# A transformer block's opening re-laid: the condition vector in eight rows, a small load moved, and a planner that may let two engines idle

## Chip, core and metric

The kernel runs on one core of one Trainium2 chip. The metric is the device time of one execution in microseconds (us); three runs of the kernel before gave 2205.80, 2207.83 and 2208.32, so a median of 2207.83. The engines are called as the profile calls them: PE (TensorE matmul; PEld is its weight load), DVE (VectorE), ACT (ScalarE), POOL (GpSimd), SP (SyncE, which issues all DMAs here).

## What is computed

One transformer block with adaptive layer norm. A condition vector `c` (1024 values) goes through silu and a matrix `w_mod` to six vectors that scale, shift and gate two halves: an attention half with 32 heads of 32 channels in four segments of 512 tokens with a running memory between them, and a token-mixing MLP half.

```python
x = A_x                                                     # (1, 2048, 1024)
mod = (_silu(c) @ w_mod).reshape(c.shape[0], 6, 1, -1)
sa, ca, ga, sb, cb, gb = (mod[:, i] for i in range(6))
h = _layernorm(x, axis=-1) * (1 + ca) + sa
x = x + ga * _A_ref(h, A_wq, A_wk, A_wv, A_wo, A_beta)
h = _layernorm(x, axis=-1) * (1 + cb) + sb
x = x + gb * _B_ref(h, B_w1, B_b1, B_w2, B_b2)
...
# in _A_ref, with g = _sigmoid(beta), one value for each head, and for each segment:
p = _softmax(logits, axis=-1); a_dot = p @ vs
o = g * (pq @ M) / (pq @ z + 1e-6) + (1.0 - g) * a_dot
M = M + pk.T @ vs; z = z + sum(pk)
```

## The kernel before

Products of fp32 operands are made as three products of fp32r halves: a helper (`split`, lines 105 to 116) writes a rounded high part (ACT, L113, or DVE, L115) and the remainder as low part (DVE or POOL, L116).

**The opening** (lines 257 to 298) does segment 0. It loads four tiles of x (L198), normalizes them in two pairs (`norm_tiles`, L205 to L222: bn_stats and bn_aggr on DVE, L212 and L213; two small ACT steps for the inverse root, L215 and L216; four small DVE steps, L217 to L220; then the scaling of each whole tile on ACT, L222). `c` comes as a 128 x 8 tile `csb` (L98), goes through silu (L99 to L103), is spread to a 128 x 1024 tile `bc` (L262), which eight PE transposes (L266) and two ACT copies (L267) turn into `scb`, in which every partition holds the whole silu(c). For each of eight chunks `ct` of 128 channels, two tiles `wm` of w_mod (512 KB each, L284) are multiplied with `scb` and summed on DVE (L285), which gives shift and scale `saca` of the chunk (L288 adds one). `h_chunk` (L224) transposes the four x tiles' columns of the chunk on PE (L227), applies scale and shift on ACT (L229) and splits the result; `first_chunk` then multiplies it with the first two head groups' weights (L182 for keys and values, L190 for queries). These weights arrive as `raw` tiles (L144) and are split. The products of all chunks go to six PSUM banks that stay open.

**The gate**: beta (32 values) is loaded to all 128 partitions (`gate`, L300, a DMA that reads the same 128 B for each partition), goes through a sigmoid on ACT and DVE (L301 to L304), and POOL makes from it eight masks `bdg` (L318 and L321, one pair for each head group), with which the memory update is multiplied when it goes into `MZ` (L429, L432). The second part of the gate (1 - g) is used where the values are scaled (L505).

**Pools**: `st1` holds the opening's tiles (x, `bc`, eleven buffers of `wm`, `h32`). `prj`, `late` and the two `sk` pools are laid over the same space once `st1` is closed, and wait tile by tile for what lay there. `gate` is in `top`, on the other side of the memory, where nothing has to be waited for.

**The order**: `set_order` hands the whole program, some 38,000 instructions, to a planner (class `Order`). It has a cost for each instruction (`cost`, `transfer`), goes through the program forward in modelled time (`forward`), then backward to get due times, three times over, and fixes the order of the instructions on each engine, SP's DMAs among them. In `forward`, `pick` takes the engine that can start something soonest and gives it the ready instruction with the smallest key (its due time); an engine does not stay idle while it has something ready (large DMAs behind a backlog apart). Each engine works its instructions off in that fixed order, so that an instruction that waits holds up what stands behind it.

Of the kernel before, what the change touches and what calls it, by code (L numbers as in the profile page):

```python
# [9 lines left out]
F32 = mybir.dt.float32  # L10
# [3 lines left out]
AF = mybir.ActivationFunctionType  # L14
ALU = mybir.AluOpType
# [4 lines left out]
S, D, H, DH, F = 2048, 1024, 32, 32, 3584  # L20
P = 128
NSEG, L = 4, 512
NK = D // P
# [21 lines left out]
def attention_and_mlp(ctx, tc, x, wq, wkv, wo, beta, w1, b1, w2, b2, c, wm_a, wm_b, out):  # L45
    nc = tc.nc
    V, A, G, T, SY = nc.vector, nc.scalar, nc.gpsimd, nc.tensor, nc.sync
# [13 lines left out]
    const = ctx.enter_context(tc.tile_pool(name="const", bufs=1))  # L61
# [9 lines left out]
    top = top_pool.__enter__()  # L71
# [4 lines left out]
    def bank(tag, bufs, name):  # L76
# [3 lines left out]
    ident = top.tile([P, P], F32, name="ident")  # L80
# [5 lines left out]
                    channel_multiplier=1)  # L86
# [8 lines left out]
    G.memset(eps, EPS)  # L95

    csb = acst.tile([P, 2, NK], F32, name="csb")
    SY.dma_start(csb[:, 0], c)  # L98
    A.activation(csb[:, 1], csb[:, 0], AF.Exp, scale=-1.0)  # L99
    V.tensor_scalar_add(csb[:, 1], csb[:, 1], 1.0)  # L100
    V.reciprocal(csb[:, 1], csb[:, 1])
    sc = const.tile([P, NK], F32, name="sc")
    V.tensor_mul(sc, csb[:, 0], csb[:, 1])  # L103

    saca = acst.tile([P, NK, 2], F32, name="saca")
    MZ = acst.tile([P, NG, 132], F32, name="MZ")
    bdg = acst.tile([P, NG, 132], F32, name="bdg")
# [150 lines left out]
    left = tc.tile_pool(name="st1", bufs=1)  # L258
    s1p = left.__enter__()
    xs = {0: [load_x(s1p, tt) for tt in range(4)]}  # L260
    bc = s1p.tile([P, NK, P], F32, name="bc")
    V.tensor_copy(bc, sc.unsqueeze(2).to_broadcast([P, NK, P]))  # L262
    for i in range(2):
        ps = bank("pj", 2, f"scps{i}")
        for j in range(4):
            T.transpose(ps[:, 128 * j:128 * j + 128], bc[:, 4 * i + j], ident)  # L266
        A.copy(scb[:, 512 * i:512 * i + 512], ps)  # L267
    first = [[bank("pj", 2, "nps0_0"), bank("pj", 2, "nps0_1"), bank("s1", 2, "qps0")],
             [bank("pv", 1, "nps1_0"), bank("ms", 1, "nps1_1"), bank("s1", 2, "qps1")]]
# [26 lines left out]
    norm_tiles(s2p, xs[1])  # L296
    for ct in range(NK):
        h_chunk(s2p, xs[1], 1, ct)
    gate = top.tile([P, 3, H], F32, name="gate")
    SY.dma_start(gate[:, 0], bass.AP(tensor=beta.tensor, offset=beta.offset, ap=[[0, P], [1, H]]))  # L300
    A.activation(gate[:, 1], gate[:, 0], AF.Exp, scale=-1.0)  # L301
    V.tensor_scalar_add(gate[:, 1], gate[:, 1], 1.0)
    V.reciprocal(gate[:, 0], gate[:, 1])
    V.tensor_scalar(gate[:, 1], gate[:, 0], -1.0, 1.0, op0=ALU.mult, op1=ALU.add)  # L304

    left.__exit__(None, None, None)
    prj = tc.tile_pool(name="prj", bufs=1, reuse_waits="tile")
    pj = prj.__enter__()
# [1 line left out]
    b = late.__enter__()  # L310
# [3 lines left out]
    skt = [[q.tile([98, 2, L], F32R, name=f"sk{i}_{h}") for h in range(4)] for i, q in enumerate(sk_)]  # L314
    for sk in skt[0] + skt[1]:
        G.memset(sk[96:98, 1].bitcast(F32), 1.0)
    for g in range(NG):
        G.tensor_tensor(bdg[:, g, 0:128].rearrange("p (h e) -> p h e", h=4),  # L318
                        bd[:, 0:128].rearrange("p (h e) -> p h e", h=4),
                        gate[:, 0, 4 * g:4 * g + 4].unsqueeze(2).to_broadcast([P, 4, 32]), op=ALU.mult)  # L320
        G.tensor_copy(bdg[:, g, 128:132], bd[:, 128:132])  # L321
# [283 lines left out]
    for n in range(-LEADS, 4 * NI + VL):  # L605
# [4 lines left out]
        if 0 <= m + 4 < 4 * NI:  # L610
            t = (m + 4) // 4
# [8 lines left out]
        if 4 * NI - 5 <= m < 4 * NI + 3:  # L620
            i = m - 4 * NI + 5
# [242 lines left out]
    for u, (ph, g) in enumerate(units):  # L864
# [59 lines left out]
        t = tp.tile([P, 3, 512], F32, tag="tu", bufs=1, name=f"tu{g}")  # L924
# [32 lines left out]
LATEB = 3000.0  # L957
HOLD = 1000.0
EARLY = 60000.0
STAY = 3000.0  # L960
SLACK = 1.06
DMA_SPREAD = 7000.0
# [115 lines left out]
class Order:  # L1078
# [182 lines left out]
    def forward(self, key):  # L1261
        n, E = len(self.X), self.E
        key = [-1e18 if i in self.follows else k for i, k in enumerate(key)]
# [8 lines left out]
        ready, start, fin, seq = [0.0] * n, [0.0] * n, [0.0] * n, []  # L1272
        free, heap, future, link = defaultdict(float), defaultdict(list), defaultdict(list), 0.0
# [9 lines left out]
        def add(i):  # L1283
# [10 lines left out]
            x = self.X[i]  # L1294
            more = HOLD if self.side(x) and ready[i] > EARLY else 0.0
            heapq.heappush(future[E[i]], (ready[i] + more, i))
# [9 lines left out]
                add(i)  # L1306
        while len(seq) < n:
            t, e, i = self.pick(free, heap, future, key)
            x = self.X[i]
            if x.opcode == "DMACopy" and size_of(x.outs[0]) > BULK and link - t - ISSUED > BACKLOG:  # L1310
                heapq.heappush(future[e], (link - ISSUED - BACKLOG, i))
                continue
            if e == "DVE" and self.C[i][2] and port > t + 300 and AVOID and heap[e]:
                near = [(k, j) for k, j in heap[e] if not self.C[j][2] and k < key[i] + AVOID]
                if near:
                    k, j = min(near)
                    heap[e].remove((k, j))
                    heap[e].append((key[i], i))
                    heapq.heapify(heap[e])
                    i, x = j, self.X[j]  # L1320
            if e == "PE":
                f = form(x)
                turn = TURNS.get(last + f, 0)
                if turn > MINT and heap[e] and i not in self.follows:
                    near = [(TURNS.get(last + form(self.X[j]), 0), k, j) for k, j in heap[e] if k < key[i] + STAY]
                    if near and min(near)[0] < turn:
                        turn, k, j = min(near)
                        heap[e].remove((k, j))
                        heap[e].append((key[i], i))
# [24 lines left out]
            for s in strong[i]:  # L1354
                done(s, t if E[s] == e == "PE" else fin[i] + WAKE.get(E[s], 30.0))
            for s in weak[i]:
                done(s, t + 1)
            for tl in tiles_of[i]:
                left[tl] -= 1
                freed[tl] = max(freed[tl], fin[i] + FREED)  # L1360
                if not left[tl]:
                    tag = self.tag_of[tl]
                    heapq.heappush(slots[tag], (freed[tl], tl))
                    again, parked[tag] = parked[tag], []
                    for s in again:
                        add(s)
# [104 lines left out]
```

## Time and profile before

| | |
|---|---|
| median of three runs | 2207.83 us |
| the profiled execution | 2210.61 us, its span 2208.9 us |
| mean granted TensorE clock | 0.998 |
| DVE busy | 1732.7 us (78%) |
| ACT busy | 1097.1 us (50%) |
| POOL busy | 725.7 us (33%) |

The span is from the first to the last record of the profiled execution; its own time has 1.7 us around the span. Times in the rows are from the span's start. A row of the timeline gives start, busy time, engine, line, operation, output and inputs, and in brackets how long the engine had been idle before and what ended that. A row of the stretches gives for each engine the busy time and the number of instructions, then the granted clock, the DMA engines' busy share and GB/s.

### The profile page before, as it was taken

What the parts mean: (1) busy time and instruction counts of PE and PEld (TensorE: products, weight loads), DVE (VectorE), ACT (ScalarE), POOL (GpSimd) and SP (SyncE); (2) the same over time, 40 slices, a digit from 0 to 9 for tenths busy, and PEclk for the clock granted to TensorE, in tenths of its full rate; (3) what the DMA queues carried; (4) which work ended last, traced back from release to release, by engine and by line L of the source; (5) the groups of instructions that cost most, each with busy time, mean ns of one, the idle gap of its engine ahead of it and who ended that gap; (6) DMA issues with size and microseconds to landing.
All of it is one profiled execution on the core that took longest, in us unless ns stands there. A gap on an engine that the chain in (4) does not pass through costs nothing.

```text
span 2208.9 us, 38272 instructions
## 1 busy us (share of the span) xinstructions
PE 2162.7 (98%) x13738; PEld 1876.5 (85%) x13738; DVE 1732.7 (78%) x3818; ACT 1097.1 (50%) x2008; POOL 725.7 (33%) x827
## 2 busy tenths in 40 slices
PE   6999999999999999989999999999999999999999
PEld 6899998989988999878878888888888888888887
DVE  8777777867787756678997555898889787878787
ACT  5688787566666665653443333633334242424232
POOL 3376676476777755551001000043321000000000
PEclk9999999999999999999999999999999999999999
DMA  9666676796777644664467555775549241414134
GB/s 370 189 204 189 192 223 196 244 288 201 224 213 235 181 135 107 191 211 157 139 238 277 191 194 197 276 278 200 201 175 337 86 157 58 149 53 148 58 124 152
DMA packets 174897, 421.74 MB, mean 191 GB/s; under 512 B 17492, under 2 KB 71796, under 8 KB 165748
## 3 DMA queue, kind: packets, MB, share of 16 engines
q1 hardware_dynamic: 174708, 419.30, 57.9%
q8 instruction: 109, 1.79, 0.3%
q14 instruction: 80, 0.66, 0.1%
HBM read 242.00 MB, written 126.37 MB: 167 GB/s over the span
## 4 chain that ended last, share of the span: by engine, by line
PE 83%; DVE 7%; POOL 2%; DMA 2%; ACT 2%; issue 1%; SPq 0%; DVEq 0%; POOLq 0%; ACTq 0%
PE mx L787 46%; PE nps L182 13%; PE qps L190 6%; PE po L688 4%; PE pv L498 4%; POOL ph L484 2%; PE a L469 1%; PE sz L445 1%; PE sx L445 1%; PE rd L417 1%; PE up L427 1%; PE a L472 1%; PE a L475 1%; PE sy L445 1%; PE ops L513 1%
## 5 line engine op out<-in xcount | busy, mean ns | idle before, releaser
L787 PE MATMUL mx<-bU,sp 128*128 128x512 f32 x2352 | 533.7, 389 | 0.9 <-DVE bU L116 0.9
L787 PEld LDWEIGHTS mx<-bU,sp 128*128 128x128 f32 x2352 | 441.3, 188 | 93.2 <-DVE bU L116 1.3
L113 ACT CAST sp<-wr 128x384 fp32r<-128x384 f32 (+2 forms) x408 | 218.4, 545 | 474.3 <-PE mx L787 386.8
L182 PE MATMUL nps<-wv,h 128*128 128x256 f32 x3072 | 444.8, 284 | 0.8 <-POOL h L116 0.6
L787 PE MATMUL mx<-bA,sp 128*128 128x512 f32 x1764 | 433.5, 389 | 1.6 <-ACT cc L792 0.7
L484 POOL TENSOR_TENSOR ph<-p,ph 128x640 f16<-128x640 f32 x256 | 385.3, 1524 | 110.1 <-ACT ph L482 109.0
L182 PEld LDWEIGHTS nps<-wv,h 128*128 128x128 f32 x3072 | 405.6, 189 | 7.0 <-POOL h L116 0.8
L787 PEld LDWEIGHTS mx<-bA,sp 128*128 128x128 f32 x1764 | 330.4, 188 | 72.7 <-ACT cc L792 1.3
L116 DVE TENSOR_TENSOR sp<-wr,sp 128x384 fp32r<-128x384 f32 (+2 forms) x408 | 260.4, 646 | 60.6 <-ACT sp L113 60.1
L794 DVE TENSOR_TENSOR ac<-mx,ac 128x512 f32<-128x512 f32 x280 | 190.7, 688 | 94.6 <-PE mx L787 93.4
L190 PE MATMUL qps<-h,wq 128*128 128x512 f32 x768 | 198.7, 400 | 0.1
L482 ACT CAST ph<-p 128x1280 f16<-128x1280 f32 x128 | 161.4, 1261 | 52.5 <-POOL p L480 51.5
L688 PE MATMUL po<-wo,ots 128*128 128x512 f32 x768 | 182.4, 392 | 0.5 <-ACT mv L125 0.5
L480 POOL TENSOR_SCALAR_AFFINE_SELECT p<-p 128x256 f32<-128x256 f32 x256 | 117.6, 469 | 188.8 <-ACT p L477 94.8
L688 PEld LDWEIGHTS po<-wo,ots 128*128 128x128 f32 x768 | 143.6, 189 | 29.8 <-ACT mv L125 0.9
L190 PEld LDWEIGHTS qps<-h,wq 128*128 128x128 f32 x768 | 140.8, 190 | 29.7 <-PE sz L445 0.5
L787 PE MATMUL mx<-bB,sp 128*128 128x512 f32 x588 | 165.9, 389 | 0.0
L446 DVE CUSTOM_DVE_ANT_0 sx<-sx,mask 128x128 f32<-128x128 f32 (+1 forms) x256 | 110.9, 434 | 69.6 <-PE sx L445 68.9
L659 POOL TENSOR_TENSOR tu<-cc 128x512 f32<-128x512 f32 x14 | 19.1, 1364 | 399.5 <-DVE cc L923 372.1
L787 PEld LDWEIGHTS mx<-bB,sp 128*128 128x128 f32 x588 | 110.4, 188 | 23.0
L498 PE MATMUL pv<-vp,ph 128*128 128x97 bf16 (+1 forms) x2560 | 117.1, 200 | 1.7 <-DVE am L505 1.0
L794 DVE TENSOR_TENSOR cc<-mx,cc 128x512 f32<-128x512 f32 x140 | 95.2, 684 | 25.6 <-PE mx L787 22.0
(179 smaller groups left out, 3258.3 us busy)
## 6 DMA issues: line engine op xcount, KB each, us to landing
sk<-sg SPq DMA_DIRECT2D x384, 128.0 KB
wr<-in_w_dram SPq DMA_DIRECT2D x28, 1024.0 KB
wr<-in_w_dram SPq DMA_DIRECT2D x32, 768.0 KB
bstu<-ucd SPq DMA_DIRECT2D x28, 768.0 KB
wv<-wsp SPq DMA_DIRECT2D x36, 512.0 KB
wsp<-wv SPq DMA_DIRECT2D x32, 512.0 KB
rawm<-in_wm_b_dram SPq DMA_DIRECT2D x32, 512.0 KB
pcd<-cc SPq DMA_DIRECT2D x14, 1024.0 KB
```

The lines of the kernel that those rows point to most:

```text
L113: A.copy(hi, src)
L116: lo_eng.tensor_tensor(lo, src, hi.bitcast(F32), op=ALU.subtract)
L182: T.matmul(ps[:, aa], h[:, j, 128 * tt:128 * tt + 128], wt[:, i, o:o + 256], start=(n == 0), stop=(n >= 6 * NK - 2), skip_group_check=True)
L190: T.matmul(ps, wt[:, i, o:o + 128], h[:, j], start=(k + n == 0), stop=(3 * k + n == 3 * NK - 1))
L446: V.tensor_tensor_reduce(o, o, mask[:, 384 - 128 * i:], 1.0, -3.0e38, op0=ALU.add, op1=ALU.max, accum_out=mx[:, h % 2, i:i + 1])
L480: G.affine_select(w, w, pattern=[[0, 2], [1, 128]], compare_op=ALU.is_ge, fill=0.0, base=0, channel_multiplier=-1)
L482: A.copy(ph[:, 0], p32)
L484: G.tensor_tensor(ph[:, 1, c], p32[:, c], ph[:, 0, c], op=ALU.subtract)
L498: T.matmul(pv[:, i, 0:w], ph[:, part, o:o + 128], d["vp"][:, j, h, 0:w], start=(n == 0), stop=(n == 19), skip_group_check=True)
L688: T.matmul(ps, os_[:, i, P * ct:P * ct + P], wop[ct, nh][:, j], start=(n == 0), stop=(n == 3 * NK - 1))
L787: T.matmul(ps, ops[q][:, i, P * k:P * k + P], b[:, j], start=(m == 0 and first), stop=(m == 3 * nk - 1), skip_group_check=True)
L794: V.tensor_tensor(d, ps, d, op=ALU.add)
```

## The change

`c` is now handed over as eight rows of 128 (`NK` is 8, `P` is 128) and is loaded to eight partitions (`cr`); the silu runs on 8 x 128 elements in place. POOL makes a selector `sel`, of which block k has ones in row k and zeros elsewhere; eight matmuls of a selector block with `cr` put each row of c to all partitions, into the same PSUM banks as before. The `c` load stands behind the four x loads in the program text (the planner sets the real order). `bc` and its copy go.

The gate, its load and its sigmoid move behind the opening, and its tile from the pool `top` to the pool `late`, which lies over the opening's tiles.

In the planner's `forward`, for the first 30 us of modelled time, DVE (up to 200 ns) and ACT (up to 100 ns) pass over the instruction that they have ready, if within that time another one becomes ready whose key is smaller by more than 200 ns and which is ready before the passed-over one would be through.

```diff
-    csb = ...; SY.dma_start(csb[:, 0], c)
-    A.activation(csb[:, 1], csb[:, 0], AF.Exp, scale=-1.0)
-    V.tensor_scalar_add(csb[:, 1], csb[:, 1], 1.0)
-    V.reciprocal(csb[:, 1], csb[:, 1])
-    sc = const.tile([P, NK], F32, name="sc")
-    V.tensor_mul(sc, csb[:, 0], csb[:, 1])
...
     xs = {0: [load_x(s1p, tt) for tt in range(4)]}
-    bc = s1p.tile([P, NK, P], F32, name="bc")
-    V.tensor_copy(bc, sc.unsqueeze(2).to_broadcast([P, NK, P]))
+    sel = s1p.tile([NK, NK, P], F32, name="sel")
+    G.memset(sel, 1.0)
+    G.affine_select(sel, sel, pattern=[[-1, NK], [0, P]], compare_op=ALU.is_equal, fill=0.0, base=0, channel_multiplier=1)
+    cr = s1p.tile([NK, 2, P], F32, name="cr")
+    SY.dma_start(cr[:, 0], c)
+    A.activation(cr[:, 1], cr[:, 0], AF.Exp, scale=-1.0)
+    V.tensor_scalar_add(cr[:, 1], cr[:, 1], 1.0)
+    V.reciprocal(cr[:, 1], cr[:, 1])
+    V.tensor_mul(cr[:, 0], cr[:, 0], cr[:, 1])
     for i in range(2):
         ps = bank("pj", 2, f"scps{i}")
         for j in range(4):
-            T.transpose(ps[:, 128 * j:128 * j + 128], bc[:, 4 * i + j], ident)
+            T.matmul(ps[:, 128 * j:128 * j + 128], sel[:, 4 * i + j], cr[:, 0], start=True, stop=True)
         A.copy(scb[:, 512 * i:512 * i + 512], ps)
...
-    gate = top.tile([P, 3, H], F32, name="gate")     # load and sigmoid, ahead of the pools prj and late
...
+    gate = b.tile([P, 3, H], F32, name="gate")       # the same load and sigmoid, in the pool late, ahead of bdg
...
+EAGER = 200.0
+WD, WA = 200.0, 100.0
+SOON = 30000.0
+WAIT = {"DVE": WD, "Activation": WA}
...
             t, e, i = self.pick(free, heap, future, key)
+            soon = WAIT.get(e, 0.0) if t < SOON else 0.0
+            if soon and future[e] and future[e][0][0] <= t + soon:
+                near = [(key[j], r, j) for r, j in future[e] if r <= t + soon]
+                k, r, j = min(near)
+                if k < key[i] - EAGER and r < t + self.C[i][0]:
+                    heapq.heappush(heap[e], (key[i], i))
+                    free[e] = r
+                    continue
...
-        "c": f("c").reshape(NK, P).T,
+        "c": f("c").reshape(NK, P),
```

More of the change, by code (lines that the diff above doesn't have):

```diff
@@ L97, in attention_and_mlp @@
     csb = acst.tile([P, 2, NK], F32, name="csb")
-    SY.dma_start(csb[:, 0], c)
-    A.activation(csb[:, 1], csb[:, 0], AF.Exp, scale=-1.0)
-    V.tensor_scalar_add(csb[:, 1], csb[:, 1], 1.0)
-    V.reciprocal(csb[:, 1], csb[:, 1])
-    sc = const.tile([P, NK], F32, name="sc")
-    V.tensor_mul(sc, csb[:, 0], csb[:, 1])
     saca = acst.tile([P, NK, 2], F32, name="saca")
@@ L298, in attention_and_mlp @@
         h_chunk(s2p, xs[1], 1, ct)
-    gate = top.tile([P, 3, H], F32, name="gate")
[L300 to L304, printed above, removed]
     left.__exit__(None, None, None)
@@ L316, in attention_and_mlp @@
         G.memset(sk[96:98, 1].bitcast(F32), 1.0)
+    gate = b.tile([P, 3, H], F32, name="gate")
+    SY.dma_start(gate[:, 0], bass.AP(tensor=beta.tensor, offset=beta.offset, ap=[[0, P], [1, H]]))
+    A.activation(gate[:, 1], gate[:, 0], AF.Exp, scale=-1.0)
+    V.tensor_scalar_add(gate[:, 1], gate[:, 1], 1.0)
+    V.reciprocal(gate[:, 0], gate[:, 1])
+    V.tensor_scalar(gate[:, 1], gate[:, 0], -1.0, 1.0, op0=ALU.mult, op1=ALU.add)
     for g in range(NG):
```

## The prediction

> **What bounds the kernel now.** The page comes first:
>
> ```profile
> span 2208.9 us, 38272 instructions
> ```
> ```profile
> PE 2162.7 (98%) x13738; PEld 1876.5 (85%) x13738; DVE 1732.7 (78%) x3818; ACT 1097.1 (50%) x2008; POOL 725.7 (33%) x827
> ```
>
> PE is idle for 2208.9 - 2162.7 = 46.2 us in all. The change can win only what it takes from this, or from time in which PE is busy but slow. So the second view is the stretches, cut at the first product of the opening and at the stages behind it:
>
> ```profile
> 0.00:22.40 22.40, 5.35 (x19) 3.38 (x20) 15.75 (x39) 11.80 (x19) 2.47 (x19) 1.00 0.87 332
> 22.40:28.00 5.60, 5.60 (x26) 5.11 (x24) 5.60 (x13) 5.30 (x10) 5.02 (x7) 1.00 1.03 410
> 28.00:50.00 22.00, 22.00 (x162) 20.67 (x161) 22.00 (x45) 8.46 (x13) 11.22 (x15) 1.00 1.03 412
> 50.00:64.00 14.00, 14.00 (x108) 13.08 (x106) 9.01 (x21) 12.07 (x22) 4.54 (x9) 1.00 0.76 222
> 64.00:82.00 18.00, 16.76 (x132) 15.66 (x130) 16.48 (x50) 8.78 (x20) 4.88 (x5) 1.00 0.91 275
> ```
>
> Before 22.4 us PE has almost no work (17 of the 46.2 us idle); from there to 64 us it is never idle. So the opening's price is the moment at which the first product starts, here:
>
> ```profile
> 22.51 0.99 PE L182 MATMUL nps<-wv,h 128*128 128x256 f32 x3
> ```
>
> What sets that moment is read from ACT alone, in order of time:
>
> ```profile
> 9.42 0.21 ACT L216 ACTIVATE mvs<-mvs 128x2 f32<-128x2 f32 x1
> 13.09 0.62 ACT L113 CAST wv<-rawv 128x512 fp32r<-128x512 f32 x1 [3.47 <-DMA rawv<-in_wkv_dram]
> 13.62 0.29 ACT L215 ACTIVATE mvs<-mvs,eps 128x2 f32<-128x2 f32 x1
> 13.81 0.60 ACT L113 CAST wv<-rawv 128x512 fp32r<-128x512 f32 x1
> 14.32 0.20 ACT L216 ACTIVATE mvs<-mvs 128x2 f32<-128x2 f32 x1
> 14.43 2.36 ACT L222 ACTIVATE x<-x,mvs 128x1024 f32<-128x1024 f32 x2
> 16.69 0.21 ACT L301 ACTIVATE gate<-gate 128x32 f32<-128x32 f32 x1
> 16.93 1.14 ACT L113 CAST wq<-rawq 128x512 fp32r<-128x512 f32 x2
> 17.97 2.37 ACT L222 ACTIVATE x<-x,mvs 128x1024 f32<-128x1024 f32 x2
> 20.91 0.78 ACT L229 ACTIVATE h<-hps,saca 128x512 f32<-128x512 f32 x1 [0.57 <-PE hps L227]
> ```
>
> ACT stands still for 3.47 us in front of a weight cast whose DMA is late, and then works without a gap until all four x tiles are scaled, at 20.34. The second pair of x tiles is scaled 1.3 us after the first (16.69 to 17.97) because its statistics come late, and DVE shows why:
>
> ```profile
> 10.57 1.29 DVE L212 BATCH_NORM_STATS2 st<-x 128x6 f32<-128x512 f32 x2 [1.58 <-DMA x<-in_x_dram]
> 11.78 0.15 DVE L217 SCALAR_TENSOR_TENSOR mvs<-mvs 128x2 f32<-128x2 f32 x1
> ...
> 15.06 0.16 DVE L217 SCALAR_TENSOR_TENSOR mvs<-mvs 128x2 f32<-128x2 f32 x1
> 15.13 1.22 DVE L285 SCALAR_TENSOR_TENSOR wm<-wm,scb 128x1024 f32<-128x1024 f32 x1
> ...
> 17.71 0.15 DVE L220 SCALAR_TENSOR_TENSOR mvs<-mvs 128x2 f32<-128x2 f32 x1
> ```
>
> Four dependent steps of 0.15 us (L217 to L220) take from 15.06 to 17.86 for the second pair, since 1.22 us products stand between them. For the first pair the ACT step ends at 9.63, yet L217 comes at 11.78, behind statistics that waited 1.58 us for the third x tile.
>
> Both DMA waits have one place:
>
> ```profile
> 2.50:5.00 2.50, 0.00 (x0) 0.00 (x0) 0.17 (x1) 0.21 (x1) 0.72 (x8) 1.00 0.98 344
> 5.00:7.50 2.50, 1.20 (x6) 1.23 (x7) 2.37 (x6) 0.07 (x1) 0.00 (x0) 1.00 0.63 153
> ```
> ```profile
> SPq L284 <- DMA gate<-in_beta_dram: 1.4, 1, 1.4
> ```
>
> Between 5 and 7.5 us the stream falls from 344 to 153 GB/s, while SP's queue stands 1.4 us behind the gate's load.
>
> **The change part by part.**
>
> *The gate's load leaves the front.* At the 410 GB/s that the stream holds from 22.4 us on, the dip costs 2.5 x (410 - 153)/410 = 1.6 us, and the stretch ahead of it 0.4. I take 1.8 us for everything behind it; bounds 1.4 (the queue's own wait) and 2.0; nothing, if the stream dips for another reason. The third x tile then lands near 8.8 instead of 10.57, the weight tile at 11.3 instead of 13.09, the first `wm` pair near 12.5 and 13.8.
>
> *The idle rule.* The first pair's chain can run straight behind L216: 9.63, four steps at 0.24 us, about as dependent steps of 0.2 us follow each other on DVE (5.03 and 5.26 in the rows of the reciprocal below), so done at 10.6, not 13.7. The second pair's takes about 0.9 us rather than 2.8. The 200 ns that DVE may idle per step are below the 0.65 us of a statistics step, so the cost is at most four gaps of 0.1 us, hidden behind PE, which waits anyway.
>
> *Together on ACT.* Scaling of pair one 10.6 to 13.0, the small ACT steps for pair two to 13.6, the two weight casts to 14.8 while the chain runs on DVE, pair two 14.8 to 17.2, transposes to 17.7, scale and cast to 19.2: first product at 19.3 instead of 22.5, **3.2 us** earlier. Bounds: with the query casts (1.14 us) still ahead of pair two and half the DMA gain, 1.5 us; with the weight casts fully in ACT's gaps, 4.3 us. `saca` follows the second `wm` product, 13.8 + 1.22 + the chain, near 16, and is covered by the scaling.
>
> *c in eight rows.* Its chain is off the path if `scb` is there when the first `wm` lands, at 12.5.
>
> ```profile
> 5.03 0.20 DVE L101 RECIPROCAL csb<-csb 128x8 f32<-128x8 f32 x1
> 5.26 0.17 DVE L103 TENSOR_TENSOR sc<-csb 128x8 f32<-128x8 f32 x1
> ```
> ```profile
> L303 DVE RECIPROCAL gate<-gate x1: 345/345/345, 22.5 to 22.5; 128x32 f32<-128x32 f32 x1
> ```
> ```profile
> 6.30 1.94 PE L266 MATMUL scps<-ident,bc 128*128 128x128 f32 x8 [6.30 <-DVE bc L262]
> ```
> ```profile
> L427 PE MATMUL up<-v,pk x16: 273/276/277, 68.9 to 73.6; 128*128 128x132 f32 x16
> ```
>
> The reciprocal grows from 8 to 128 elements per partition; 143 ns more for 24 more elements makes 0.9 us (0.35 to 0.92), the two other DVE steps and the exp perhaps 0.1 us each; the 0.69 us copy to `bc` goes. A transpose was one PE record; eight true fp32 products of `up` (two updates of four) left sixteen, so the eight selector products cost about twice 1.94 us. The last transpose ends at 8.24, and the second copy to `scb` 0.6 us later, near 8.9; this becomes 8.9 - 0.7 + 1.0 + 1.9 = 11.1, less if eight rows of 512 B land sooner than 128 of 32 B. That is 1.4 us of cover. If the load slips behind all x loads, the cover is gone and up to 2 us return. POOL's selector (a memset and one select over 1024 columns) has no row of this size; its nearest is a mask's 1.04 us for 128 columns, so up to eight times that by columns, 0.2 us from below (the shortest DVE steps); POOL has 20 us free ahead of 22.4, and at 2 us the selector is ready when the first product needs it. I take 0 for this part, bounds 0 and +2.
>
> *The gate behind the opening.* Its tile now lies over the first `wm` buffer, so it waits for the twelfth of the sixteen `wm` products (an estimate of 40 us, three quarters of the way from 15 us to the end of DVE's full stretch at 50), and SP's issues behind it wait with it; the first that PE needs are the `sk` loads (L339 to L341) of the first attention step, which cannot be issued before keys and queries are done. I count this wait as covered. The POOL work moves with it:
>
> ```profile
> L318 POOL TENSOR_TENSOR bdg<-bd,gate 128x128 f32<-128x128 f32 x8 | 8.3, 1036 | 19.5 <-DVE gate L303 19.5
> L321 POOL COPY bdg<-bd 128x4 f32<-128x4 f32 x8 | 7.3, 915 | 0.0
> ```
> ```profile
> L429 DVE TENSOR_TENSOR MZ<-up,bdg x8: 278/288/296, 77.1 to 441.0; 128x132 f32<-128x132 f32 x8
> ```
> ```profile
> 70.15 1.72 POOL L116 TENSOR_TENSOR h<-h,h 128x512 fp32r<-128x512 f32 x1
> ```
> ```profile
> L116 DVE TENSOR_TENSOR h<-h,h x5: 679/819/883, 23.8 to 37.8; 128x512 fp32r<-128x512 f32 x5
> ```
>
> That is 15.6 us of POOL, from 23 to 38 us before, now from about 48 on (load, sigmoid and the longer landing of such a load), where POOL has 9.5 of 14 us free; the first mask is needed only at 77. It can hold up one `h` remainder on POOL by at most one piece (1.04 us), and DVE's own remainders grow by 0.2 us (883 against 679 ns, the longer ones while POOL makes masks), which they now are spared in the opening. I take **+0.3 us**, bounds -1.2 (PE's idle time from 64 to 82) and the price of the third rival.
>
> The Trainium skill's page "SBUF — State Buffer", section "Who interferes with whom", speaks against this move: a VectorE step with two SBUF inputs and a GpSimd step that reads SBUF exclude each other for the whole instruction, so that masks laid into a busier DVE stretch cost DVE a mask's full time. By that rule the estimate for two such hits would be +2.1 rather than +0.3 us; the row shows 0.2 us a hit, and I go by the row.
>
> **Sum.** -3.2 + 0 + 0.3 = -2.9 us on the profiled 2210.61 us (2208.9 of span and 1.7 around it), so 2207.7 there. This execution was 2.8 us above the median of 2207.83; the same 2.9 us on the median give **2204.9**.
>
> **Rivals.**
>
> *More than that (2202.3).* The opening wins its bound of 4.3, and DVE, spared nine hits of 0.2 us and 1.8 us earlier fed, is ahead of PE at 64 to 82 us, where PE's 1.24 us idle go: -5.5. For it: ACT's gap is 3.47 us alone. Against it: ACT's own rows from 13.09 to the last scaling hold over 7 us of work, whatever their order.
>
> *The slow stretch stays (2206.1).* From 22.4 to 28 us PE makes 26 records in 5.6 us, then 162 in 22: 4.6 against 7.4 a microsecond, though the granted clock reads 1.00. If this stretch ends at a fixed moment and not a fixed time after the start, the 3.2 us are won at 4.6/7.4 of their worth: -2.0 + 0.3. The Trainium skill's page "TensorE: Matmul & The Clock Gate", section "What's actually happening", tells of an activity window of about 3.4 us that runs free of the kernel, by which the end of the stretch may move by a whole window or not at all; that is this case, or one as much better. No row of one execution can tell.
>
> *The moved gate bites (2213.5).* The planner lays the 15.6 us of masks ahead of the four `h` remainders on POOL. If the gate lands late, say masks from 56 us, they end at 71.6, and four remainders of 1.5 us behind them at 77.6; the last ended at 71.87 and would be 3.2 us earlier. That is 8.9 us late, -3.2 + 8.9 = +5.7. It is slower than before from 3.2 us of delay on. Against it: the planner knows these due times, and the first mask is not due until 77.
>
> *That the change does not do what it says* (the small steps still apart, only the DMA gain left, -1.8) gives 2206.0 and is counted with the second rival.
>
> **How the numbers follow.** The forecast 0.38 (own range 2202.8 to 2206.8), more than that 0.34, the slow stretch or no idle effect 0.16, the gate 0.12. What a measurement of this kernel tells from no change is about 0.2%, 4.4 us: faster is below 2203.4, slower above 2212.2. Faster: 0.34 + 0.06 from the forecast's low end = 0.40. Slower: 0.08 of the gate's 0.12. Within: 0.52. The range reaches from 2200.5 (a part of the first rival lies below, since a newly laid order shifts small waits all along the 2200 us) to 2209.0 (above lies most of the third).
>
> **What would show it.** Right: no dip at 5 to 7.5 us; the third x tile's statistics near 9; L217 to L220 within 1.2 us each time; ACT's wait for the weight tile gone; the first product near 19.3; slow stretch of about 5.6 us from there; masks on POOL from about 48 us, and no new wait on POOL at 58 to 75. Wrong: `scb` later than the first `wm`; a first product after 21; an idle PE between 25 and 60; a wait for `gate` or `bdg` in PE's or DVE's rows; or a change of idle time far behind 100 us that is larger than that of the opening.

## The result, and the profile after

The changed kernel takes **2235.99 us** (median of four runs, 2235.27 to 2236.57) against 2207.07 for the kernel before in the same comparison (2205.80 to 2208.32): a ratio of 1.0131, 95% interval 1.0113 to 1.0148. It is slower by 28.9 us, where the prediction had it faster by 2.9.

The page's first lines of the changed kernel, span and engines' busy time:

```profile
span 2233.6 us, 38287 instructions
```
```profile
PE 2193.4 (98%) x13746; PEld 1879.9 (84%) x13746; DVE 1735.8 (78%) x3817; ACT 1097.8 (49%) x2008; POOL 715.7 (32%) x829
```

Put beside the same two lines of before, they hold most of the answer. PE's idle time, span less busy time, was 2208.9 - 2162.7 = 46.2 us and is 2233.6 - 2193.4 = 40.2: it fell by 6.0, as a better opening would have it. PE's **busy** time rose by 30.7 us, with eight records more. 30.7 - 6.0 = 24.7 us is the whole difference of the two spans. So PE waits less in all; its products themselves have become slower.

Which ones is seen in the groups of instructions of PE (busy time, then mean ns of one; products overlap in the pipe, so the mean of one is longer than the step to the next). Before, three groups with the same form, 128 x 128 by 512:

```profile
L787 PE MATMUL mx<-bU,sp 128*128 128x512 f32 x2352 | 533.7, 389 | 0.9 <-DVE bU L116 0.9
...
L190 PE MATMUL qps<-h,wq 128*128 128x512 f32 x768 | 198.7, 400 | 0.1
L688 PE MATMUL po<-wo,ots 128*128 128x512 f32 x768 | 182.4, 392 | 0.5 <-ACT mv L125 0.5
```

and after (the lines have moved up by one to seven):

```profile
L786 PE MATMUL mx<-bU,sp 128*128 128x512 f32 x2352 | 549.2, 395 | 0.0
...
L183 PE MATMUL qps<-h,wq 128*128 128x512 f32 x768 | 197.7, 399 | 0.2
L687 PE MATMUL po<-wo,ots 128*128 128x512 f32 x768 | 183.2, 394 | 0.0
```

`mx` are the products of the MLP, 2352 of this group and 2352 more with `bA` and `bB`. This group alone grew by 15.5 us; `qps` and `po` changed by 1 us at most, one down and one up. The products with `bA` grew by 10.7 us, those with `bB` by 2.5 (before, then after):

```profile
L787 PE MATMUL mx<-bB,sp 128*128 128x512 f32 x588 | 165.9, 389 | 0.0
```
```profile
L786 PE MATMUL mx<-bB,sp 128*128 128x512 f32 x588 | 168.4, 393 | 0.0
```

The diff doesn't touch line 787. The chain of waits within 50 us of the MLP (start, length, what, how many) makes the pace exact; first before, then after:

```profile
1799.99 50.12 PE mx L787 x221
```
```profile
1799.89 50.17 PE mx L786 x215
```

50.12 / 221 = 226.8 ns from one product to the next, and 50.17 / 215 = 233.3: 6.5 ns more, without a gap in either. The granted clock reads 1.00 in both stretches:

```profile
1250.00:1300.00 50.00, 50.00 (x223) 41.39 (x222) 28.47 (x40) 17.62 (x31) 0.00 (x0) 1.00 0.56 201
```
```profile
1250.00:1300.00 50.00, 50.00 (x217) 40.30 (x216) 27.59 (x39) 17.03 (x30) 0.00 (x0) 1.00 0.57 200
```

The first `mx` starts at 1133.74 us before and 1131.13 after, 2.6 us earlier; the last at 2204.13 and 2228.82. Between the two lie 1070.4 and 1097.7 us: +27.3. -2.6 + 27.3 = +24.7, all of the difference.

What the diff does to the MLP is not in its instructions but in its **addresses**. Tiles are laid one behind another; the pool `const` lies at the start of the left side and stays open to the end. With the tile `sc` it lost 32 B per partition, and so the later tiles of the left side, those of the MLP among them, slid down by 32 B. On the right side the MLP's tiles stayed (some of the attention stage's moved by the 384 B of the gate's tile). In the built programs the MLP's stationary tiles `sp` went from 1728 to 1696, while the moving tiles `bA` and `bU` stayed at 143296 and up. The two operands had started at the same place modulo 256 B, and are 32 B apart now. `po` has both operands on the left: both moved, and its pace stayed. The moving tiles `bB` lie on the left too and moved with `sp`; that their 588 products got slower all the same is taken up behind the table below.

The opening after, in the same stretches as before:

```profile
0.00:22.40 22.40, 8.65 (x34) 6.81 (x35) 17.00 (x40) 13.23 (x21) 4.38 (x21) 1.00 0.88 338
22.40:28.00 5.60, 5.60 (x35) 5.25 (x34) 5.60 (x12) 3.17 (x6) 0.00 (x0) 1.00 1.03 410
...
64.00:82.00 18.00, 16.44 (x132) 15.47 (x132) 15.80 (x42) 8.31 (x21) 9.02 (x17) 1.00 0.87 280
...
5.00:7.50 2.50, 1.38 (x6) 1.42 (x7) 2.13 (x4) 0.00 (x0) 0.30 (x4) 1.00 0.84 282
```

The dip at 5 to 7.5 us has gone from 153 to 282 GB/s. PE does more ahead of 22.4 us (8.65 against 5.35 us busy), but 3.75 us of this are the new selector products, where the transposes took 1.94. PE's timeline shows them, and the first product behind them:

```profile
6.12 3.75 PE L266 MATMUL scps<-cr,sel 8*128 8x128 f32 x16 [6.12 <-DVE cr L262]
...
21.64 1.20 PE L175 MATMUL nps<-wv,h 128*128 128x256 f32 x4
```

It starts at 21.64 us, not at 19.3. ACT in order of time shows why (start, busy, and in brackets the idle time and what ended it):

```profile
9.90 0.59 ACT L267 COPY scb<-scps 128x512 f32<-128x512 f32 x1 [1.12 <-PE scps L266]
10.62 0.30 ACT L208 ACTIVATE mvs<-mvs,eps 128x2 f32<-128x2 f32 x1
10.95 0.21 ACT L209 ACTIVATE mvs<-mvs 128x2 f32<-128x2 f32 x1
...
13.01 2.36 ACT L215 ACTIVATE x<-x,mvs 128x1024 f32<-128x1024 f32 x2
16.09 2.37 ACT L215 ACTIVATE x<-x,mvs 128x1024 f32<-128x1024 f32 x2 [0.73 <-DVE mvs L213]
18.38 1.12 ACT L106 CAST wq<-rawq 128x512 fp32r<-128x512 f32 x2
19.40 1.44 ACT L222 ACTIVATE h<-hps,saca 128x512 f32<-128x512 f32 x2
```

The wait for the weight tile has shrunk from 3.47 us to 0.51. But now the second copy to `scb` waits 1.12 us for the selector products and ends only at 10.49, and the first pair's inverse root (L208, L209), which ended at 9.63 before, stands behind it and ends at 11.16. Pair two's scaling waits 0.73 us for L213, the last of its four small steps:

```profile
12.38 0.16 DVE L213 SCALAR_TENSOR_TENSOR mvs<-mvs 128x2 f32<-128x2 f32 x1
...
13.53 0.16 DVE L212 SCALAR_TENSOR_TENSOR mvs<-mvs 128x2 f32<-128x2 f32 x1
13.61 1.22 DVE L285 SCALAR_TENSOR_TENSOR wm<-wm,scb 128x1024 f32<-128x1024 f32 x1
...
15.90 0.16 DVE L213 SCALAR_TENSOR_TENSOR mvs<-mvs 128x2 f32<-128x2 f32 x1
```

Three of the steps run together, and two 1.22 us products stand in front of the fourth.

### The profile page after: what moved, and what is told of

Its sections match the earlier page's. It is cut to its first block, busy times and chain, and to the rows that moved or that the text cites. A ratio compares the mean times of both kernels' runs of the same rounds, so it can differ in the third digit from the quotient of the medians.

```text
span 2233.6 us, 38287 instructions
## 1 busy us (share of the span) xinstructions
PE 2193.4 (98%) x13746; PEld 1879.9 (84%) x13746; DVE 1735.8 (78%) x3817; ACT 1097.8 (49%) x2008; POOL 715.7 (32%) x829
## 4 chain that ended last, share of the span: by engine, by line
PE 88%; DVE 4%; POOL 2%; DMA 2%; ACT 2%; issue 1%; SPq 0%; DVEq 0%; POOLq 0%
PE mx L786 49%; PE nps L175 14%; PE po L687 7%; PE qps L183 6%; PE pv L497 4%; PE a L468 1%; PE sz L444 1%; PE sx L444 1%; POOL ph L483 1%; PE rd L416 1%; PE up L426 1%; PE a L471 1%; PE a L474 1%; PE ops L512 1%; DMA rawm<-in_wm_b_dram 1%
## 5 line engine op out<-in xcount | busy, mean ns | idle before, releaser
L786 PE MATMUL mx<-bU,sp 128*128 128x512 f32 x2352 | 549.2, 395 | 0.0
L786 PE MATMUL mx<-bA,sp 128*128 128x512 f32 x1764 | 444.2, 395 | 1.4 <-ACT sp L106 0.6
L658 POOL TENSOR_TENSOR tu<-cc 128x512 f32<-128x512 f32 x14 | 19.3, 1377 | 409.7 <-DVE cc L922 384.0
```

Source lines behind the costliest of these rows:

```text
L786: T.matmul(ps, ops[q][:, i, P * k:P * k + P], b[:, j], start=(m == 0 and first), stop=(m == 3 * nk - 1), skip_group_check=True)
```

## The experiments

The expectations call the theories by letters. **A** is that the addresses of the operands make the MLP slower; A1 that the distance between the two operands decides, A2 that the place of one of them does. The rivals are named in each. A kernel with one run is read by its chain of waits and by the distance from the first `mx` to the last, where the change's 27.3 us stand against a scatter of 2 us (1068.4 to 1070.4 in all kernels whose MLP operands start equal); the whole time of the kernel before lies between 2203.47 and 2212.93 us over all comparisons.

### The addresses alone set back

```diff
+    const.tile([P, NK], F32, name="pad3")
```

The pad goes into the changed kernel, in the place of `sc`; nothing uses it.

> The changed kernel with an unused tile of 32 B per partition in the pool const, where the 32 B of sc were before, so that all tiles on the left side of the memory lie as in the kernel before; everything else is the change. Theory A (addresses: sc went, the weight tiles sp slid by 32 B against a 64 B grid, and each of the 4704 MLP products mx takes 233 ns instead of 227): mx products start 227 ns apart again, the time falls from 2236 to about 2205 (the 2.6 us won ahead of the first mx product stay). Rival B (the newly laid order of the MLP's instructions sets the slower pace): about 2236, products still 233 ns apart.

2206.33 us (11 runs, 2204.64 to 2209.09), ratio to before 0.9995, 95% interval 0.9986 to 1.0004. The chain:

```profile
1799.96 50.12 PE mx L787 x221
```

226.8 ns again. The two programs have the same order of instructions on every engine; they differ only in that the left side's tiles lie 32 B higher with the pad. So the planner's new order is not the cause. All that the change adds in time comes back with 32 B that no instruction touches; what is left of it can't be told from no change.

### The kernel before, moved off

Two ways to make the kernel before slow, without any part of the change. First, `sc` in another pool:

```diff
-    sc = const.tile([P, NK], F32, name="sc")
+    sc = acst.tile([P, NK], F32, name="sc")
```

> The kernel before with sc taken from the pool const into the pool acst: no part of the change but the missing 32 B in const. Theory A: sp slides to 32 past a multiple of 64 B, mx products 233 ns apart, time about 2207 + 4704 x 0.0062 = 2236. Rival B (order, or the opening's other edits): 2207, products 227 ns apart.

2243.68 us (one run): 36 us lost by the place of one 32 B tile. From first to last `mx` it takes 1097.7 us, as in the changed kernel. Here it loses some 6 us more ahead of the MLP: the first `mx` starts at 1139.51, against 1133.74 in the profile of before. Since `acst` grew where `const` shrank, the weights behind it stayed while the pages with `h` moved, and so the distances in `nps` and `qps` changed too.

Second, `sp` moved by 32 B, with a second pad behind it. The pools that lie behind both pads move by 64 B, `yb` with the tiles `bB` among them:

```diff
     sp = ctx.enter_context(tc.tile_pool(name="sp", ...))
+    sp.tile([P, 8], F32, name="pad3")
...
     yb = ctx.enter_context(tc.tile_pool(name="yb", ...))
+    yb.tile([P, 8], F32, name="pad4")
```

> The kernel before with 32 B of padding at the head of the pool sp and 32 B more at the head of yb, so that of all matmul operands only the weight tiles sp (stationary) lie 32 past a multiple of 64 B, and only in the MLP; moving operands bA, bB, bU stay on the grid. Theory A: 233 ns, about 2236, and so the stationary operand alone is enough. Rival B, or if it is another tile that slid (page, ots, yb): 227 ns, 2207.

2238.23 us (one run), 1097.6 us from first to last `mx`, and nothing ahead of it changed (`po` starts at 927.47, before 928.21). So it is enough to move `sp` and what lies behind it; the constants, the pages and the attention stage's weights need not move. Of what moved, the products with `bA` and `bU` read `sp` alone. That some other engine's access to the pools that moved by 64 B slows them is not excluded by this run.

### Distance or place

The changed kernel with the right side's tiles, `bA` and `bU` among them, slid by 32 B as well, by a wider pad at the right edge:

```diff
-    edge.tile([P, 8], F32, name="pad")
+    edge.tile([P, 16], F32, name="pad")
```

> The changed kernel with 32 B more padding at the edge of the right side, so that the moving tiles bA and bU too lie 32 past a multiple of 64 B, as sp and bB do. Theory A1 (what counts is that stationary and moving operand lie differently on the 64 B grid, as the products po of the output projection say, both operands 32 off and 227 ns in either kernel): mx at 227 ns, about 2205. Theory A2 (a stationary operand off the grid is slow by itself): 233 ns, about 2236. Rival B: 233 ns, 2236.

2204.80 us (one run), and the chain:

```profile
1799.92 50.11 PE mx L786 x221
```

Both operands are off by 32 B and the pace is the good one: A1, the distance counts. The same edit in the kernel before moves the right side alone, `bA` and `bU` with it:

> The kernel before with 32 B more padding at the edge of the right side: the MLP's moving tiles bA and bU lie 32 past a multiple of 64 B, the stationary sp and the moving bB on it. Theory A1 (a difference between the two operands): 233 ns wherever bA or bU moves, about 2236. Theory A2' (only a stationary operand off the grid of its moving one costs, or a stationary one off the grid): 227 ns, 2207.

2235.42 us (one run), 1096.8 us from first to last `mx`. A place of the moving operand that was fine in the run above is slow here; that leaves A1.

### Which distances

The kernel before again, pad of 24 and of 40 elements, so that `bA` and `bU` lie 64 and 128 B lower:

> The kernel before, with 64 B more in front of the moving tiles of the MLP on the right side of the memory (the pad of the pool edge is 24 instead of 8 elements wide), so bA and bU start 64 B lower per partition and sp stays. Theory A (the two operands' starts are compared modulo 64 B): MLP products at 226.7 ns from start to start, time about 2207 us, as before. Rival (they are compared modulo 128 B or more, the 32 B case being only one of the slow ones): 231 to 235 ns, about 2235 us.

2233.44 us (one run). The rival held: 64 B is as bad as 32.

> The kernel before with the moving tiles of the MLP 128 B lower (pad of 40 instead of 8 elements in edge), sp unmoved. Theory A with a grid of 128 B: MLP products at 226.7 ns, time about 2207 us. Theory A with a grid of 256 B: 231 to 235 ns, time 2233 to 2236 us as with 32 and 64 B.

2229.55 us (one run), a little less, not the good pace:

```profile
1799.85 50.32 PE mx L787 x216
```

50.32 / 216 = 233.0 ns here; the median over all its `mx` is 231. So of the distances tried only 0 modulo 256 is good for the MLP's products.

If equal starts are best, `nps` and `qps` should win by them: their operands are 192 and 64 B apart, in the kernel before too. This is the try at a version better than both:

```diff
     aw = paw.__enter__()
+    aw.tile([P, 16], F32, name="pad4")
...
     s1p = left.__enter__()
+    s1p.tile([P, 48], F32, name="pad5")
...
     pj = prj.__enter__()
+    pj.tile([P, 48], F32, name="pad6")
```

> The changed kernel with the addresses of e1, and three more pads (64 B ahead of the projection weights wv and wq, 192 B behind them, so that nothing else moves by other than 256 B): the two operands of the products nps (before 192 B apart, modulo 256) and qps (64 B apart) now start equal modulo 256. Theory A (the operands' starts are compared modulo 128 or 256 B, for every product of this kind): nps from 116 to 117 ns to about 113.3 (half of 226.7), qps from 230 to 231 to about 227; over 3072 and 768 products 8 + 3 = 11 us at most, time 2195 to 2199 us, ratio to before 0.995 to 0.997, if the attention stage is bound by PE there. Rival (only the MLP's products are sensitive, or what costs 3 ns in nps is something else): spacings and time as in e1, about 2206 us.

2213.37 us (7 runs, 2209.93 to 2215.71), ratio 1.0031, 95% interval 1.0020 to 1.0043: slower by some 7 us, where 11 were to be won. The group of `nps` in the kernel with the one pad, then here:

```profile
L176 PE MATMUL nps<-wv,h 128*128 128x256 f32 x3072 | 443.0, 284 | 1.4 <-POOL v L354 0.8 <-POOL h L110 0.5
```
```profile
L177 PE MATMUL nps<-wv,h 128*128 128x256 f32 x3072 | 451.6, 287 | 1.4 <-POOL v L357 0.7 <-POOL h L110 0.5
```

`nps`, with 256 columns, got slower by equal starts; `qps`, with 512, a little faster (the median step went from 231 ns to 227, the mean by 1). So the distance works on all three kinds of product that were tried, and the best of the distances tried isn't the same for both widths. The table has the mean of the steps from the start of a product to the start of the next one of its group (all `mx` are one group) where that stands right behind it, without those that stand at a wait (over 300 ns, for `nps` over 160); the first column is of the steps that begin with an `mx` product with `bA` or `bU`, the second of those that begin with one with `bB`. Distance is moving less stationary start, modulo 256 B:

```
kernel                 mx bA, bU: dist., mean   mx bB: dist., mean   first to last mx   qps: dist., mean   nps: dist., mean
before                         0   226.8 ns          0   226.8 ns    1070.4 us           64   231.5 ns     192   116.1 ns
after                         32   233.3             0   231.4       1097.7              64   231.9        192   116.2
after, pad (e1)                0   226.8             0   226.8       1069.4              64   231.8        192   116.2
before, no sc (e2)            32   233.3             0   231.4       1097.7              32   234.7        224   118.4
before, sp +32 (e3)          224   233.2            32   233.3       1097.6              64   231.5        192   116.2
after, all 32 (e4)             0   226.8             0   226.8       1068.9              64   231.8        192   116.2
before, b 32 (e5)            224   233.4             0   228.8       1096.8              64   231.5        192   116.2
before, b 64 (e6)            192   233.3             0   230.3       1097.0              64   231.7        192   116.2
before, b 128 (e12)          128   232.3             0   230.3       1093.1              64   231.7        192   116.2
after, aligned (e11)           0   226.8             0   226.8       1069.0               0   230.9          0   119.5
```

The second column is an open end. The 588 products with `bB` stand, mostly by threes, among those with `bA`. Their own two operands are 0 apart in all these kernels but e3, and yet they slow down, to 228.8 to 231.4 ns, wherever the products with `bA` do. So a product's own distance is not the whole rule. That the products beside it count too would fit, and no run tests it.

### The opening, part by part

These four are made from the changed kernel with the addresses set back, so the MLP is as before in each.

**Without the idle rule:**

```diff
-WAIT = {"DVE": WD, "Activation": WA}
+WAIT = {}
```

> The changed kernel with the 32 B of padding in const, and the planner's idle rule off; the rest of the change stays. If the rule is worth what the forecast gave it (chains of the small steps unbroken), the first pair's four steps stretch from 0.7 to over 2 us again and the first product comes about 1 us later than the 21.3 of the padded kernel; the time 0.5 to 1 us longer, 2207. If the rule is worth nothing here: first product within 0.4 us of 21.3, time unchanged at 2206.

2214.97 us (5 runs), ratio 1.0030, interval 1.0018 to 1.0042, against 0.9995 with the rule. The four steps of the second pair on DVE, and ACT behind them:

```profile
14.69 0.16 DVE L211 SCALAR_TENSOR_TENSOR mvs<-mvs 128x2 f32<-128x2 f32 x1
14.76 1.22 DVE L286 SCALAR_TENSOR_TENSOR wm<-wm,scb 128x1024 f32<-128x1024 f32 x1
...
18.33 0.16 DVE L214 SCALAR_TENSOR_TENSOR mvs<-mvs 128x2 f32<-128x2 f32 x1
```
```profile
18.53 1.24 ACT L216 ACTIVATE x<-x,mvs 128x1024 f32<-128x1024 f32 x1 [2.11 <-DVE mvs L214]
```

Each of the last three steps has a 1.22 us product in front of it, ACT waits 2.11 us, and the first product starts at 24.23 us instead of 21.25, 3.0 us late. The first `mx` is 9.2 us late (1138.71 against 1129.49); the other 6 us arise between the opening and the MLP, where this run has another order too; they are not taken apart here.

**The gate's load at the front again** (its lines and its pool `top` as before):

> The changed kernel with the padding, and the gate's load, sigmoid and tile where they were before; the rest of the change stays. Forecast's theory: the dip to about 130 GB/s between 5 and 7.5 us is back, the first weight tile lands 1 to 1.8 us later, and so does the first product (22.3 to 23); masks on POOL from about 23 us. Rival (front DMA not on the path any more, since ACT waits for the second copy to scb): first product at 21.3 to 21.7, time unchanged.

2207.80 us (11 runs), ratio 0.9996, interval 0.9987 to 1.0005.

```profile
5.00:7.50 2.50, 0.91 (x4) 0.94 (x5) 2.43 (x5) 0.00 (x0) 0.34 (x4) 1.00 0.64 129
```

The dip is back, so the gate's load makes it. The first weight cast comes 0.7 us later (12.04 against 11.30). But the first product starts at 21.15 us, against 21.25 without the load: the data that it holds up is not what the path waits for by now.

**The old way of c** (`csb`, `sc`, `bc` and the eight transposes of before; gate and idle rule as in the change):

> The changed kernel with c in 128 x 8 as before, spread by bc and eight transposes (so with sc in const, no further padding); gate behind the opening and idle rule stay. Theory: the selector products, twice as long, put the second copy to scb at 10.4 on ACT, and the first pair's inverse root behind it (10.86 instead of 9.1); with the old spread that copy is at 8.3, the inverse root near 9.1, and the first product 1 to 1.7 us earlier (19.6 to 20.3), the time near 2205. Rival (c off the path, as forecast): first product at 21.3, 2206.

2209.30 us (12 runs), ratio 1.0003, interval 0.9995 to 1.0011. Its ACT:

```profile
8.34 0.59 ACT L266 COPY scb<-scps 128x512 f32<-128x512 f32 x1 [0.27 <-PE scps L265]
10.06 0.30 ACT L214 ACTIVATE mvs<-mvs,eps 128x2 f32<-128x2 f32 x1 [1.14 <-DVE mvs L212]
...
15.45 2.37 ACT L221 ACTIVATE x<-x,mvs 128x1024 f32<-128x1024 f32 x2 [0.88 <-DVE mvs L219]
```

The second copy to `scb` starts 1.6 us earlier than in the changed kernel, and the first product at 20.99, only 0.3 to 0.7 us earlier, since the inverse root then waits 1.14 us for the statistics. So little lies within what single profiles of one opening scatter (1.6 us, below), and the time is no shorter: that the selector products cost anything on the path is not shown.

**A planner that knows what the selector products take** (each costed at 223 instead of 111 ns, and `EAGER` at 0, so that it waits for any earlier due time):

```diff
-EAGER = 200.0
+EAGER = 0.0
...
-            held = 223 if c in (132, 1) else 111
+            held = 223 if c in (132, 1) or m.ap[0][1] == NK else 111
```

> The changed kernel with its addresses set back (the pad of e1), EAGER at 0 instead of 200 ns, and the eight selector products costed by the planner at 223 ns instead of 111. MLP products stay at 226.7 ns. If what holds the opening back is that the planner breaks the second pair's chain and thinks the second scb copy earlier than it is: chain of the second pair unbroken, first product at 20 to 21 us instead of 21.25, time 2203 to 2206 us, ratio to before 0.998 to 0.9995. If the order in the opening is worth nothing by now (the slow stretch and the later order decide): first product within 0.5 us of 21.25 or earlier, time 2205 to 2209 us, ratio 0.9990 to 1.0005.

2207.97 us (11 runs), ratio 1.0001, interval 0.9992 to 1.0010. The second pair's four steps run unbroken (15.55 to 16.30), but two products and two weight remainders now stand ahead of all four, ACT waits 1.41 us for them, and the first product starts at 22.61. It was no better version. None of these runs makes one that is shown to be faster than the kernel before.

## Why the prediction was wrong, point by point

**The failed step: a cost that the list didn't hold.** "The change part by part" went through what the diff issues: instructions, DMAs, queues, waits. In *c in eight rows* it wrote "I take 0 for this part, bounds 0 and +2" and counted the steps on DVE, ACT and PE; that the same lines take a 32 B tile out of a pool that lies under everything on the left side was not priced. "-3.2 + 0 + 0.3" took for granted that all behind the opening runs as it did. Moving one operand by 32 B was worth +27.3 us over 4704 products; the run with the pad shows the addresses as cause, and those with one side or the other moved show that the distance of the two operands counts, and not the place of one.

The moved addresses could have been read from the two programs before any run; what they cost could not. The rows of before hold a hint: two groups of one form with different means, `mx` at 389 ns and `qps` at 400, in a kernel with two tiles named `pad` that nothing reads.

The prediction's list of what would prove it wrong looked for "a change of idle time far behind 100 us". Time could also change as **busy** time, and did.

**The opening: -3.2 was mis-sized.** The single profile of before starts its first product at 22.51 us. Five other runs that have this opening unchanged (the kernels e2, e3, e5, e6 and e12) start it at 20.89 to 22.18; with the profile of before the mean of the six is 21.7. The changed opening has 21.64, 21.25 and 21.32 (after, e1, e4), a mean of 21.4. At the first `mx` the same means are 1132.0 (without e2, whose attention stage is slower) and 1130.0. By these averages the new opening won 0.3 us at its own end and some 2 by the MLP, not 3.2 and 2.9, and both lie within the scatter of single profiles (1.6 and 4 us). The sum started from 22.51, of which 0.8 us were that one execution's. What kept the first product from 19.3 is on ACT: the second copy to `scb` ahead of the first pair's inverse root, and the wait for L213. Taken as times, the run with the pad gives -0.9 us, between -3.1 and +0.9 by its interval.

- *The gate's load leaves the front*: the dip goes, and comes back with the gate, so this much was right. The 1.8 us were not. In the six profiles of the old opening, all with a dip to 113 to 153 GB/s, the first weight cast starts between 11.48 and 13.09 us, at 12.3 in the mean, so that 0.8 of the 13.09 were that execution's own; in the new opening the load moves that cast by 0.7 us and the first product not at all (e8).
- *The idle rule*: right that a broken chain costs ACT its wait. Without the rule, the first product is 3.0 us later in the new opening. But the chains weren't unbroken as forecast: the first took 0.7 us as hoped, yet began only at 11.84, and the second was broken ahead of L213.
- *c in eight rows*: the reciprocal took 0.94 us (forecast 0.9), the selector's memset and select 0.94 and 1.08 (forecast bounds 0.2 and eight times 1.04). The selector products took 3.75 us (forecast twice 1.94), and the second copy ended at 10.49, ahead of the 11.1 reckoned. What the step missed is that this copy stands on ACT's queue ahead of the first pair's inverse root: the cover was reckoned against the first `wm` product, which was not the first to suffer.
- *Together on ACT*: the query casts (1.12 us) came between pair two's scaling and `h`, where the lower bound had them ahead of pair two, and two scalings of `h` came before its first cast.

**The moved gate did no harm**, so the third rival's price didn't fall due, and nothing speaks against +0.3. The groups of the masks and their first use, then DVE's and POOL's rows beside them:

```profile
L317 POOL TENSOR_TENSOR bdg<-bd,gate x8: 392/396/851, 60.7 to 70.0; 128x128 f32<-128x128 f32 x8
...
L428 DVE TENSOR_TENSOR MZ<-up,bdg x8: 278/286/296, 75.6 to 438.9; 128x132 f32<-128x132 f32 x8
```
```profile
61.76 1.74 DVE L109 TENSOR_TENSOR h<-h,h 128x512 fp32r<-128x512 f32 x1
...
65.62 1.76 DVE L109 TENSOR_TENSOR h<-h,h 128x512 fp32r<-128x512 f32 x1
...
69.90 0.68 DVE L109 TENSOR_TENSOR h<-h,h 128x512 fp32r<-128x512 f32 x1
```

The gate's load goes out at 38.2 us, near the 40 of the forecast, but its sigmoid begins only at 57.9, and the masks come at 60.7 rather than 48. They take 0.4 us each mostly rather than 1.04, and are done 4 us before their first use. Two of DVE's `h` remainders took 1.74 and 1.76 us instead of 0.68, each while POOL made an `h` remainder of its own with masks around it. That is 1.07 us a hit, five times the 0.2 us that I took from the row of the opening. But it was POOL's remainder and not a mask that they met: both ended 0.55 us after it (at 62.95 and 66.83). The kernel before has such a hit with no mask near. The step shown here takes 0.69 us at 78.27, but 1.78 beside a POOL remainder that starts at 66.50:

```profile
66.95 1.78 DVE L405 TENSOR_TENSOR vp<-r,vp 128x512 bf16<-128x512 f32 x1
```

So it is not shown that the moved masks cost DVE these 2 us. The Trainium skill's page "SBUF — State Buffer", section "Who interferes with whom", by which such steps exclude each other for the whole instruction, gave +2.1 us for two hits of a mask; the rows agree with the exclusion, and that 2 x 1.07 comes to the same 2.1 is luck. PE hardly felt it: its idle time from 64 to 82 us went from 1.24 to 1.56 us.

**The slow stretch** behind the first product lasted 5.7 us before and 3.1 after, from the first product to the first two `nps` less than 150 ns apart. Over all runs it lasted 1.6 to 5.7 us and ended between 22.8 and 28.2 us. It is a stretch at half clock, although the rows of the stretches read 1.00 there: each trace's record of the clock begins only within the last 0.9 us of the slow stretch (at 27.98 us before, 24.73 after), and a time without a record counts as 1.00. Ahead of that moment two `nps` start 213 ns apart, behind it 113 to 117. Further on, where half clock is on record, the same is seen: in the stretch shown here, of the changed kernel, two `po` start 427 ns apart, elsewhere 227.7.

```profile
957.00:959.90 2.90, 2.90 (x9) 2.31 (x8) 1.97 (x4) 1.97 (x3) 1.20 (x2) 0.50 0.92 298
```

So the prediction read the 1.00 as more than it says. In the six profiles of the old opening the record begins anywhere from 24.03 to 27.98 us, so that neither a fixed end nor a fixed length holds, and 3 us at the end of the stretch are chance from run to run. The Trainium skill's page "TensorE: Matmul & The Clock Gate", section "What's actually happening", speaks of a window that runs free of the kernel; such a scatter agrees with this, and so do the stretches of half clock behind the opening, which last 3.41 us each (6.83 in two).

## What to carry to other kernels

When a change adds or drops a tile, however small, compare the addresses of the operands of the longest products before and after, and try the change once with a pad in the place of the lost tile: only that comparison tells the change's own worth from that of the layout. In the profile the sign is a higher busy time and a higher mean of a group that the diff doesn't touch, with no new wait. And a term of 3 us at the start of a kernel can't be taken from one profile where the same code starts its first product over a range of 1.6 us.

## What the runs showed of the hardware that was not expected

- The pace of back-to-back fp32r products depends on where their operands start within a partition, one against the other. For 512 columns: 226.8 ns at a distance of 0 modulo 256 B in the MLP, 232.3 to 233.4 at 32, 128, 192 and 224. For 256 columns the order is another: 116.1 to 116.2 ns at 192, 118.4 at 224, 119.5 at 0.
- The place of one operand alone doesn't decide: with both 32 B off, the pace is 226.8 ns.
- At the start of a trace a granted clock of 1.00 can stand for a time without a record: the pace there was that of half clock (213 ns against 113 to 117).
- Open: by what mechanism, why the width matters, and why the products with `bB` slow down at a distance of 0. That the load of the next weights and the stream of the moving operand meet in some part of the memory was not tested; nor were other distances for 256 columns, of which one might be better than 192.
